# One core, two spectral layers and two feed-forward layers: the input loaded tile by tile, its 16-point matrix on another queue, and a new order table

## The chip, the cores and the metric

The kernel runs on 1 core of one Trainium2 chip. The metric is the device time in microseconds, lower is better. The core has TensorE (PE, and PEld for its weight loads), VectorE (DVE), ScalarE (ACT), GpSimd (POOL) and SyncE (SP). SP's and ACT's instruction streams issue transfers on a queue of their own (SPq, ACTq); GpSimd issues indirect ones.

## The reference

The input x has 2048 rows of 448 bf16 numbers. Two kinds of layer alternate, twice:

```python
def _A_ref(x, w_r, w_i):                       # spectral layer
    X = rfft2(x.astype(float32))               # over 2048 x 448
    return irfft2(X * (w_r + 1j * w_i), s=(2048, 448)).astype(bfloat16)

def _B_ref(x, w1, b1, w2, b2):                 # feed-forward layer, 448 -> 1792 -> 448
    r = relu(x @ w1 + b1)
    return (r * r) @ w2 + b2

x = x + _A_ref(layernorm(x), A_w_r, A_w_i)
x = x + _B_ref(layernorm(x), B_w1, B_b1, B_w2, B_b2)
x = x + _A_ref(layernorm(x), A_w_r, A_w_i)
x = x + _B_ref(layernorm(x), B_w1, B_b1, B_w2, B_b2)
```

## The kernel before, in words

x lies in 16 tiles of 128 partitions x 448; partition p holds rows 16p to 16p+15, and tile t their t-th. The transform over 2048 rows is split into 16 x 128 points. All of it is matrix products with constant matrices.

The first stage ("A1") works tile by tile. VectorE (BN_STATS, then BN_AGGR) or, for tiles 1, 4 and 6, ScalarE (one pass with Copy, one with Square, each with a running sum) takes the mean and variance; ScalarE takes the square root; VectorE its reciprocal (`rstd`). The function `minus` writes -2 times the mean (`m2`). The function `scaled` multiplies the 16-point matrix FA by rstd into a buffer `Fs`. Then come five matmuls: four with x as weights and the scaled matrix as the moving operand, and one with m2 that takes the mean out. These five are called a product here. An evacuation writes the result from PSUM to `XA`. There are four Fs buffers in rotation, so the scaling of tile t waits until the product of tile t-4 has read its buffer.

After that, for eight pairs of frequencies: TD (a transform over the 448 columns, constant TD_sb), B (the 128-point transform, G_sb), W (VectorE's products with the complex weights Wt) and Bi (the transform back, H_sb or HS_sb). TI and AI (TI_sb, FI_sb) finish the way back and add the residual. Then per pair of tiles a layer norm and a transposition into yT (by matmuls with J_sb, or by a transposing transfer), then the first feed-forward matrix (`h`) and the second (`o`). The second half of the kernel repeats all that, with its first stage ("A2") woven into the feed-forward stage.

Every instruction is recorded with what it reads and writes. Instructions that go together form a unit with a tag ("A1.3", "sp.xin"). The table `ORDER` gives each unit of a tag, in the order in which the program recorded them, its rank, and a letter for the engine where there is a choice. Each engine runs its instructions strictly by rank, and so does each queue its transfers. Before the change, `schedule` also keeps a clock of its own with costs and due times, by which it chooses a PSUM bank for each matmul tile and puts dummy matmuls (`warm_mm`, on a block of ones) where it finds TensorE idle while the array would be slow.

Names that the prediction uses: `xin` is the input in SBUF, `x_sb` the running x, whose rows are 512 wide. `x4` is the tile whose landing the constants' transfers wait for. ACT's `warm` instruction is a square root of one number, which makes ScalarE load its table of functions.

Of the kernel before, what the change touches and what calls it, by code (L numbers as in the profile page):

```python
# [10 lines left out]
P = 128  # L11
# [30 lines left out]
def make_constants():  # L42
# [71 lines left out]
    for g, M in enumerate((cl * np.cos(th), cl * np.sin(th))):  # L114
# [1270 lines left out]
```

## Time and profile before

| what | value |
|---|---|
| median of 3 runs | 267.37 us (266.88 to 268.2) |
| span of the profiled execution | 267.8 us |
| instructions | 5840 |
| DMA, whole execution | 17.03 MB, mean 64 GB/s |
| TensorE's granted clock, mean | 1.000 |

The page gives the span of the profiled execution, from its first to its last instruction, and no other time for it. The profile's rows for a stretch of time show the start and length in microseconds, the engine, the line, the operation with what it writes and reads, the count, and in brackets the idle time of the engine just before and what ended it. The rows of busy times by stretch show the length and then, for TensorE, its weight loads, VectorE, ScalarE and GpSimd, the busy time and the number of instructions, then the granted clock, the busy share of the DMA engines and the GB/s they moved. The granted clock stands at 1.00 in all these rows; how fast the array works is read from the distance between the starts of matmuls.

### The profile page before, as it was taken

The numbers are of one execution on the slowest core, as the hardware profiler recorded it, in microseconds if no ns is written. First come the engines' busy times: TensorE is split into PE (matmuls) and PEld (weight loads), VectorE is DVE, ScalarE is ACT, GpSimd is POOL, SyncE is SP. The second block draws the span as 40 slices with busy tenths as digits, with TensorE's granted clock in tenths as the row PEclk, the third lists the DMA queues.
The fourth block names the chain that finished last, engine by engine and source line by source line (L and its number), as shares of the span: only waits on it lengthen the run. The fifth ranks groups of instructions, "written<-read, shape, count | busy, mean of one in ns | idle before, by whom it ended". The sixth has DMA issues, their size and how long they took to land. (4 is left out here: it accounts for less than half of the span.)

```text
span 267.8 us, 5840 instructions
## 1 busy us (share of the span) xinstructions
PE 259.3 (97%) x2194; PEld 158.9 (59%) x2194; DVE 212.7 (79%) x652; ACT 171.3 (64%) x391; POOL 14.4 (5%) x42
## 2 busy tenths in 40 slices
PE   6899999899999999999999999989999999999996
PEld 1477665798544544555559774779654554454554
DVE  5866999899996964999999899899998963463722
ACT  4688994979429755985128896889735753678000
POOL 0577000000000000000000000000000000000000
PEclk9999999999999999999999999999999999999999
DMA  6999370020420222300000000011232026200211
GB/s 222 305 376 354 74 228 17 0 42 10 54 52 2 39 43 44 68 0 0 2 0 4 2 2 0 2 23 22 39 73 42 0 42 111 89 2 0 70 39 47
DMA packets 27312, 17.03 MB, mean 64 GB/s; under 512 B 20210, under 2 KB 25810, under 8 KB 27156
## 3 DMA queue, kind: packets, MB, share of 16 engines
q1 hardware_dynamic: 26692, 14.82, 21.7%
q10 hardware_dynamic: 432, 1.03, 1.1%
q0 software_dynamic: 160, 0.81, 0.8%
q8 instruction: 17, 0.28, 0.5%
q14 instruction: 11, 0.09, 0.1%
HBM read 11.15 MB, written 1.84 MB: 48 GB/s over the span
## 5 line engine op out<-in xcount | busy, mean ns | idle before, releaser
L636 PE MATMUL ps<-yT,W_sb 64*128 64x512 bf16 (+1 forms) x770 | 90.3, 346 | 0.0
L636 PE MATMUL ps<-W_sb,arena 128*128 128x448 bf16 (+2 forms) x490 | 87.5, 336 | 0.0
L636 PEld LDWEIGHTS ps<-yT,W_sb 64*128 64x128 bf16 (+1 forms) x770 | 51.5, 95 | 36.0 <-issue 1.5
L636 PEld LDWEIGHTS ps<-W_sb,arena 128*128 128x128 bf16 x490 | 46.3, 98 | 36.3 <-DVE arena L688 0.8
L655 ACT ACTIVATE arena<-ps,b1col 128x512 bf16<-128x512 f32 x84 | 51.9, 691 | 14.2 <-PE ps L636 14.0
L688 DVE TENSOR_TENSOR arena<-arena 128x512 bf16<-128x512 bf16 (+1 forms) x140 | 45.7, 367 | 18.0 <-ACT arena L655 17.6
L1109 ACT ACTIVATE VT<-x_sb 128x448 bf16<-128x448 bf16 x32 | 18.4, 577 | 13.4 <-DVE x_sb L1085 13.3
L661 ACT ACTIVATE arena<-ps 128x448 bf16<-128x448 f32 (+1 forms) x44 | 25.1, 693 | 2.4 <-PE ps L636 2.2
L1205 DVE SCALAR_TENSOR_TENSOR x_sb<-ps,arena 128x448 bf16<-128x448 f32 (+2 forms) x27 | 15.2, 570 | 14.1 <-PE ps L636 13.7
L655 ACT ACTIVATE mv<-mv,epst 128x1 f32<-128x1 f32 (+1 forms) x46 | 12.6, 294 | 17.2 <-DVE mv L794 12.1
L655 ACT ACTIVATE arena<-ps 128x256 bf16<-128x256 f32 x56 | 17.8, 392 | 4.0 <-PE ps L636 3.7
L661 ACT ACTIVATE XA<-ps 128x512 bf16<-128x512 f32 x29 | 15.6, 592 | 3.2 <-PE ps L636 3.2
L661 ACT ACTIVATE VT<-ps 128x512 bf16<-128x512 f32 (+1 forms) x26 | 13.0, 567 | 7.0 <-PE ps L636 6.9
L636 PE MATMUL ps<-yT,VT 64*128 64x512 bf16 x42 | 15.8, 376 | 0.0
L636 PE MATMUL ps<-HS_sb,arena 128*128 128x512 bf16 x64 | 14.9, 380 | 0.1
L636 PE MATMUL ps<-arena,G_sb 128*128 128x448 bf16 (+1 forms) x76 | 14.4, 333 | 0.5 <-ACT arena L661 0.4
L672 ACT ACTIVATE arena<-x_sb,rstd 128x448 bf16<-128x448 bf16 x11 | 7.2, 666 | 10.5 <-DVE rstd L1124 6.0
L636 PE MATMUL ps<-TD_sb,XA 112*64 112x112 bf16 (+2 forms) x312 | 13.2, 224 | 0.0
L636 PE MATMUL ps<-Fs,xin 128*128 128x256 bf16 x64 | 10.0, 290 | 3.0 <-DVE mv L784 2.9
L636 PEld LDWEIGHTS ps<-TD_sb,XA 112*64 112x64 bf16 (+2 forms) x312 | 12.1, 108 | 1.1 <-issue 0.6
L688 DVE TENSOR_TENSOR tmp<-arena,Wt 128x896 bf16<-128x896 bf16 (+1 forms) x14 | 11.4, 852 | 1.7 <-ACT arena L661 1.5
L1135 DVE SCALAR_TENSOR_TENSOR arena<-x_sb,mv,b2row 128x448 bf16<-128x448 bf16 x16 | 10.7, 679 | 0.1
(76 smaller groups left out, 300.9 us busy)
## 6 DMA issues: line engine op xcount, KB each, us to landing
out_dram<-x_sb SPq DMA_DIRECT2D x15, 112.0 KB, 1.7
W_sb<-in_B_w_dram SPq DMA_DIRECT2D x1, 1568.0 KB, 16.1
W_sb<-in_B_w_dram SPq DMA_DIRECT2D x1, 1344.0 KB, 6.7
HS_sb<-c_HS SPq DMA_DIRECT2D x1, 1024.0 KB, 11.2
G_sb<-c_G SPq DMA_DIRECT2D x1, 960.0 KB
xin<-in_A_x_dram ACTq DMA_DIRECT2D x2, 448.0 KB, 5.4
xin<-in_A_x_dram SPq DMA_DIRECT2D x1, 448.0 KB
Wt<-in_A_w_i_dram SPq DMA_DIRECT2D x1, 392.0 KB, 4.7
```

The costliest lines, as they stand in the source:

```text
L636: return sch.add("pe", lambda e: e.matmul(_res(o), lhsT, rhs, start=start, stop=stop, skip_group_check=skip), [lhsT, rhs], [o], cost=cost, ...
L655: sch.add("act", lambda e: e.activation(o, _res(i), func, **kw), rd, [o], cost=c)
L661: op = sch.add(engs[0], lambda e: e.activation(o, _res(i), ACT.Copy) if h[0].eng == "act" else e.tensor_copy(o, _res(i)), [i], [o], cost=c ...
L672: op = sch.add(engs[0], lambda e: e.activation(o, i, ACT.Copy, scale=s) if h[0].eng == "act" else e.tensor_scalar(o, i, s, 1.0, op0=ALU.mu ...
L688: sch.add(eng, lambda e: e.tensor_tensor(o, _res(a), b, op), [a, b], [o], cost=_free(o) / rate + 69.0)
L1109: sch.add("act", lambda e, i=i, o=o, x=x: e.activation(o, x, ACT.Square, accum_out=mv[:, i, 4:5]), [x], [o, mv[:, i, 4:5]], cost=560.0)
L1135: small(lambda e, o=o, x=x, m=m: e.scalar_tensor_tensor(out=o, in0=x, scalar=m, in1=b2row[:], op0=ALU.add, op1=ALU.add), [x, m, b2row[:]], ...
L1205: small(lambda e: e.scalar_tensor_tensor(out=o, in0=_res(i), scalar=r[0] if r else 1.0, in1=xb[:, t, d0:d1], op0=ALU.mult, op1=ALU.add), [ ...
```

## The change

Four things are changed in the text, and one table.

1. x is loaded in 12 pieces in place of 7: tiles 0 to 7 one by one, the rest in pairs, divided between SP's and ACT's queue. FA goes on ACT's queue.
2. The scaled matrix of tile t is written to `x_sb[:, t, 0:256]`, a place of its own, in place of one of four buffers in rotation.
3. The dummies are listed in a table: 13 of 512 columns and one of 128, ahead of the first product. Before it was nine ahead of the first product and seven between the first and the second.
4. The constants' transfers wait for tile 7, where they waited for tile 4 (which came with 5, 6 and 7).
5. ORDER is new up to the beginning of the first feed-forward stage, and from there on has the old order with all ranks five higher. It now also holds the PSUM bank of each matmul tile (after the colon), so `schedule` only follows the table.

```diff
 ORDER = {
-    "dve.warm": "1", "dve.epst": "4", "sp.xin": "0 12 15 18", "act.xin": "11 14 17", "sp.FA_sb": "13",
+    "dve.warm": "170", "dve.epst": "12", "sp.xin": "17 14 29 10 15 13 11", "act.xin": "7 5 4 0 1", "act.FA_sb": "2",
-    "act.warm": "16", "pool.ones": "8", "pool.back": "10", "dve.x_sb": "3", "dve.W1_sb": "5", "pool.yT": "92 52",
+    "act.warm": "202", "pool.ones": "8", "pool.back": "9", "dve.x_sb": "3", "dve.W1_sb": "6", "pool.yT": "25 24",
...
+WARM = {52: ((7, 512), (7, 512), (7, 512), (7, 512), (7, 512), (7, 512), (7, 512), (7, 512), (7, 512), (7, 512), (7,
+    512), (7, 512), (7, 512), (7, 128))}
...
-        for u in self.ranked():
-            e = u.eng
...
+        for n, u in enumerate(self.ranked()):
+            for b, w in WARM.get(n, ()):
+                d = _Op("pe", self.warm_fn(b, w), False, 0.0, 0.0)
+                take(b, d)
...
-        for n, (a, b, e) in enumerate(((0, 1, "sp"), (1, 2, "act"), (2, 3, "sp"), (4, 8, "act"), (3, 4, "sp"), (8, 12, "act"),
-                                       (12, 16, "sp"))):
+        for n, (a, b, e) in enumerate(((0, 1, "sp"), (1, 2, "act"), (2, 3, "sp"), (3, 4, "sp"), (4, 5, "act"), (5, 6, "sp"),
+                                       (6, 7, "act"), (7, 8, "sp"), (8, 10, "sp"), (10, 12, "act"), (12, 14, "sp"),
+                                       (14, 16, "act"))):
             dma(e, xin[:, a:b, :], x_dram[:, a:b, :])
-            if n == 2:
-                dma("sp", FA_sb[:], dc["FA"])
-            if n == 3:
+            if n == 1:
+                dma("act", FA_sb[:], dc["FA"])
                 sch.add("act", lambda e: e.activation(warm[:, 0:1], warm[:, 0:1], ACT.Sqrt), [warm[:, 0:1]], [warm[:, 0:1]],
                         cost=200.0)
...
-        x4 = [xin[:, 4, :]]
+        x4 = [xin[:, 7, :]]
...
-                x, f = xin[:, t, :], Fs[:, t % NFS, :]
+                x, f = xin[:, t, :], x_sb[:, t, 0:2 * P]
                 scaled(f, FA_sb[:], r, EV["FS"])
```

Three places show what the new table does at the start. The names in brackets are the semaphores that an instruction waits for; `s_sp_dma5` is that of the sixth transfer on SP's queue, counted from 0.

SP's transfers at the start of the program, before:

```order
L628 DMA xin<-in_A_x_dram 128x448 x2
L628 DMA FA_sb<-c_FA 128x256
L628 DMA xin<-in_A_x_dram 128x448
L628 DMA xin<-in_A_x_dram 128x1792
L628 DMA G_sb<-c_G 128x768 [waits s_act_dma1]
L628 DMA Wt<-in_A_w_i_dram 128x2x224
L628 DMA Wt<-in_A_w_i_dram 128x7x224
L628 DMA TD_sb<-c_TD 128x896
```

These are tiles 0 and 2, FA, tile 3, tiles 12 to 15, then the constants. And now, with tile 5, the pairs 12-13 and 8-9, tiles 2, 7 and 0, and behind TD tile 3:

```order
L550 DMA xin<-in_A_x_dram 128x448
L550 DMA xin<-in_A_x_dram 128x896 x2
L550 DMA xin<-in_A_x_dram 128x448 x3
L550 DMA TD_sb<-c_TD 128x896 [waits s_sp_dma4]
L550 DMA xin<-in_A_x_dram 128x448
L550 DMA Wt<-in_A_w_r_dram 128x7x224
L550 DMA G_sb<-c_G 128x3840
```

Tile 0 moved from the first place to the sixth, tile 3 behind a transfer that waits for tile 7.

ScalarE's first instructions, with its queue's transfers (tile 1, tiles 4 to 7, tiles 8 to 11), before:

```order
L628 DMA xin<-in_A_x_dram 128x448
L628 DMA xin<-in_A_x_dram 128x1792
L729 ACT_TABLE_LOAD
L729 ACTIVATE warm<-warm 128x1 [waits s_dve]
L628 DMA xin<-in_A_x_dram 128x1792
L781 ACTIVATE yT,mv<-xin 128x448 [waits s_act_dma0]
L655 ACTIVATE mv<-mv,epst 128x1 [waits s_dve]
```

And now, with the pairs 10-11 and 14-15, FA, then tiles 6, 4 and 1:

```order
L550 DMA xin<-in_A_x_dram 128x896 x2
L550 DMA FA_sb<-c_FA 128x256
L550 DMA xin<-in_A_x_dram 128x448 x3
L701 ACT_TABLE_LOAD
L701 ACTIVATE yT,mv<-xin 128x448 [waits s_act_dma5]
L577 ACT_TABLE_LOAD
L577 ACTIVATE mv<-mv,epst 128x1 [waits s_dve]
```

Tile 1 moved from the first place to the sixth, and a table load now stands between tile 1's first pass and the square root for tile 0 (`mv<-mv,epst`).

VectorE from its first statistics to the first scaled matrix, before:

```order
L793 BN_STATS st<-xin 128x6 [waits s_sp_dma0]
L794 BN_AGGR mv<-st 128x2 [waits s_dve]
L793 BN_STATS st<-xin 128x6 [waits s_sp_dma1]
L794 BN_AGGR mv<-st 128x2 [waits s_dve]
L800 RECIPROCAL rstd<-mv 128x1 [waits s_act]
L805 TENSOR_SCALAR m2<-mv 128x1
L673 TENSOR_SCALAR Fs<-FA_sb,rstd 128x256 [waits s_dve,s_sp_dma2]
```

And now:

```order
L713 BN_STATS st<-xin 128x6 [waits s_sp_dma5]
L714 BN_AGGR mv<-st 128x2 [waits s_dve]
L713 BN_STATS st<-xin 128x6 [waits s_sp_dma3]
L720 RECIPROCAL rstd<-mv 128x1 [waits s_act]
L713 BN_STATS st<-xin 128x6 [waits s_sp_dma7]
L714 BN_AGGR mv<-st 128x2 [waits s_dve]
L713 BN_STATS st<-xin 128x6 [waits s_sp_dma0]
L714 BN_AGGR mv<-st 128x2 [waits s_dve]
L704 SCALAR_TENSOR_TENSOR mv<-mv 128x1 [waits s_act]
L714 BN_AGGR mv<-st 128x2 [waits s_dve]
L720 RECIPROCAL rstd<-mv 128x1 [waits s_act]
L595 TENSOR_SCALAR x_sb<-FA_sb,rstd 128x256 [waits s_act_dma2]
```

The scaled matrix of tile 0 (last row) now stands behind the statistics of tiles 0, 2, 3 (`s_sp_dma7`) and 5 (`s_sp_dma0`), where it stood behind those of tiles 0 and 2.

More of the change, by code (lines that the diff above doesn't have):

```diff
@@ L327 @@
     DMA_RATE = 350.0
-    TURN = (200.0, 100.0)
-    SLACK = 60.0
-    DMA_SLACK = 200.0
-    BEGIN = 800.0
-    WINDOW = 3413.0
     def __init__(self):
@@ L342, in __init__ @@
         self.lead = {}
-        self.warm_from = 0.0
-        self.cold_until = 0.0
-        self.warm_share = 0.7
     def add(self, eng, fn, reads=(), writes=(), is_dma=False, cost=100.0, lat=130.0, unit=None):
@@ L403, in ranked @@
             if u.tag in ORDER:
-                w = ORDER[u.tag].split()[k]
+                w = ORDER[u.tag].split()[k].split(":")
+                for t, b in zip(u.tiles, w[1] if len(w) > 1 else ""):
+                    t.bank = int(b)
+                w = w[0]
                 if w[-1].isalpha():
@@ L415, in schedule, with take @@
     def schedule(self):
-        free = dict.fromkeys(self.ENGINES, self.BEGIN)
-        free["pe"] = self.warm_from
-        bank_free = [0.0] * NB
-        bank_user = [None] * NB
-        dma_free = 0.0
-        rows = 128
-        used = []
-        done = {}
-        def ready(op):
-            r = 0.0
-            for d in op.gdeps:
-                if d.unit is op.unit or (d.eng == "pe" and op.eng == "pe"):
-                    continue
-                if d.is_dma:
-                    r = max(r, done[d] + 130.0 + self.DMA_SLACK)
-                else:
-                    r = max(r, done[d] + d.lat + (80.0 if op.eng == "pe" else 0.0) + (self.SLACK if d.eng != op.eng else 0.0))
-            return r
-        def pick(n, now, taken):
-            best = None
-            for b in range(0, NB, n):
-                if any(i in taken for i in range(b, b + n)):
-                    continue
-                if all(bank_user[i] is None or all(op in done for op in bank_user[i].readers) for i in range(b, b + n)):
-                    f = max(bank_free[b:b + n])
-                    key = (max(f, now), n == 1 and bank_free[b ^ 1] <= now, f)
-                    if best is None or key < best[0]:
-                        best = (key, b)
-            assert best is not None, "no bank is free"
-            return best[1]
-        for u in self.ranked():
-            e = u.eng
-            first = free[e] + (self.TURN[u.rows < 128] if e == "pe" and u.rows != rows else 0.0)
-            taken = []
-            for w in u.tiles:
-                now = max(first, ready(u.ops[0])) + sum(op.cost for op in u.ops[:u.ops.index(w.first)])
-                w.bank = pick(w.n, now, taken)
-                taken += range(w.bank, w.bank + w.n)
+        user = [None] * NB
+        def take(b, op):
+            if user[b] is not None:
+                op.deps.extend(r for r in user[b].readers if r not in op.deps)
+        for n, u in enumerate(self.ranked()):
+            for b, w in WARM.get(n, ()):
+                d = _Op("pe", self.warm_fn(b, w), False, 0.0, 0.0)
+                take(b, d)
+                if not self.ops["pe"]:
+                    d.deps.extend(self.warm_deps)
+                self.ops["pe"].append(d)
             for op in u.ops:
-                t = max(first if op is u.ops[0] else free[e], ready(op))
                 for w in u.tiles:
@@ L461, in schedule @@
                         for i in range(w.bank, w.bank + w.n):
-                            old = bank_user[i]
-                            if old is not None:
-                                t = max(t, bank_free[i] + 80.0 + self.SLACK)
-                                for rd in old.readers:
-                                    if rd not in op.deps:
-                                        op.deps.append(rd)
-                            bank_user[i] = w
-                if e == "pe" and op is u.ops[0]:
-                    while t - free["pe"] >= 120.0:
-                        f = free["pe"]
-                        cold = f < self.cold_until
-                        recent = sum(min(b, t) - max(a, t - self.WINDOW) for a, b in used[-90:] if b > t - self.WINDOW)
-                        if not (cold or recent < self.warm_share * self.WINDOW):
-                            break
-                        n = next((n for n in (512, 256, 128) if (n / 2.4 + 2.5) * (2.0 if cold else 1.0) + 60.0 <= t - f), 0)
-                        if not n:
-                            break
-                        b = min(((bank_free[b], b) for b in range(NB) if b not in taken and (
-                            bank_user[b] is None or all(x in done for x in bank_user[b].readers))), default=None)
-                        if b is None:
-                            break
-                        if b[0] > f:
-                            free["pe"] = b[0]
-                            continue
-                        c = (n / 2.4 + 2.5) * (2.0 if cold else 1.0)
-                        d = _Op("pe", self.warm_fn(b[1], n), False, c, 195.0)
-                        if bank_user[b[1]] is not None:
-                            d.deps.extend(bank_user[b[1]].readers)
-                        if not self.ops["pe"]:
-                            d.deps.extend(self.warm_deps)
-                        self.ops["pe"].append(d)
-                        used.append((f, f + c))
-                        free["pe"] = f + c
-                    t = max(t, free["pe"])
-                    begin = t
@@ L497, in schedule @@
-                t += op.cost
-                free[e] = t
-                done[op] = t
-                self.ops[e].append(op)
-                if op.is_dma:
-                    done[op] = dma_free = max(dma_free, t + 1800.0) + op.lat
-                    if e == "pool":
-                        done[op] = max(dma_free, t + 7000.0)
-                for w in op.takes:
-                    for i in range(w.bank, w.bank + w.n):
-                        bank_free[i] = max(bank_free[i], t + op.lat)
@@ L508, in schedule @@
-            if e == "pe":
-                rows = u.rows
-                used.append((begin, free["pe"]))
-        self.length = max(done.values())
-        self.used = used
-        self.done = done
+                            take(i, op)
+                            user[i] = w
+                self.ops[u.eng].append(op)
         for e in self.ENGINES:
@@ L732, in bass_interleave_layers__spectral_gfnet__dense_activation_squared_relu__prompt_kernel @@
         sch.warm_deps = sch.lead["pool"] = [sch.last_write[k] for k in _pages(ones[:])][:1]
-        sch.warm_from = 1000.0
-        sch.cold_until = 4800.0
         sch.add("pool", lambda e: e.iota(back[:, 0:1], pattern=[[0, 1]], base=(16 * (P - 1) + 9) * 225, channel_multiplier=-16 * 225), [],
```

191 rows, old and new, of the table ORDER are left out of this document.

## Prediction

> **What bounds the kernel now.** I read the busy shares first, then the chain that ended last, then TensorE's busy time by stage, and at last the first 21 us row by row, because that is where the diff works.
>
> ```profile
> PE 259.3 (97%) x2194; PEld 158.9 (59%) x2194; DVE 212.7 (79%) x652; ACT 171.3 (64%) x391; POOL 14.4 (5%) x42
> ...
> 175.25 90.26 PE ps L636 x700
> ```
>
> The last row is a piece of the chain that ended last (start, length, who): its final 90 us are matmuls in a row. A busy TensorE need not be TensorE at its peak, so I ask where it stood still.
>
> ```profile
> 13.00:21.15 8.15, 8.10 (x72) 6.62 (x70) 5.34 (x21) 6.62 (x15) 5.13 (x14) 1.00 1.03 374
> 21.15:46.14 24.99, 24.38 (x179) 15.76 (x177) 22.43 (x37) 19.79 (x39) 4.96 (x13) 1.00 0.58 164
> 46.14:62.00 15.86, 15.08 (x166) 13.35 (x165) 13.92 (x40) 13.65 (x39) 0.00 (x0) 1.00 0.09 18
> 60.00:70.00 10.00, 10.00 (x80) 7.64 (x79) 9.80 (x36) 8.20 (x27) 0.00 (x0) 1.00 0.29 29
> ```
>
> These are stretches from the span's start: length, then busy time of TensorE, weight loads, VectorE, ScalarE, GpSimd. TensorE lacks 0.05 us in the first, 24.99 - 24.38 = 0.61 in the second, 15.86 - 15.08 = 0.78 in the third, and nothing from 60 on. So from 13 us to the feed-forward stage TensorE is the bound, with only 0.61 + 0.78 = 1.39 us to be had from a better order. A start that shifts the first stage shifts everything behind it.
>
> **The start before.** TensorE's rows of the first stage (start, length, engine, line, operation, count, idle before):
>
> ```profile
> 0.98 4.02 PE L1307 MATMUL ps<-ones 128*128 128x512 bf16 x9 [0.98 <-POOL ones L709]
> 7.95 1.01 PE L636 MATMUL ps<-Fs,xin 128*128 128x256 bf16 x4 [2.95 <-DVE mv L784]
> 8.97 3.19 PE L1307 MATMUL ps<-ones 128*128 128x512 bf16 x7
> 11.96 1.06 PE L636 MATMUL ps<-Fs,xin 128*128 128x256 bf16 x4
> 12.81 0.38 PE L636 MATMUL ps<-Fs,m 128*128 128x256 bf16 x1
> 13.02 0.60 PE L636 MATMUL ps<-Fs,xin 128*128 128x256 bf16 x4
> 13.57 0.60 PE L636 MATMUL ps<-Fs,xin 128*128 128x256 bf16 x4
> ...
> 21.15 2.46 PE L636 MATMUL ps<-TD_sb,XA 128*128 128x224 bf16 x24
> ```
>
> The nine dummies follow each other by about 0.43 us. The first product (five matmuls, tile 0) takes 8.97 - 7.95 = 1.02 us; from 13.02 on one takes 13.57 - 13.02 = 0.55. So the array runs at half pace until about 12.8, that is for 12.8 - 7.95 = 4.85 us of unbroken work, and the nine dummies before the 2.95 us pause left no trace of speed at 7.95. The products end, and the next transform starts, at 21.15. The same stage for the other engines and queues:
>
> ```profile
> 0.72 0.87 SPq L628 DMA_DIRECT2D xin<-in_A_x_dram  x2
> 1.64 0.43 SPq L628 DMA_DIRECT2D FA_sb<-c_FA  x1
> 1.65 1.28 ACT L729 ACT_TABLE_LOAD   x1 [1.65 <-PEq L1370]
> 3.31 0.63 DVE L793 BATCH_NORM_STATS2 st<-xin 128x6 f32<-128x448 bf16 x1 [0.28 <-DMA xin<-in_A_x_dram]
> 3.50 0.58 ACT L781 ACTIVATE yT<-xin 128x448 bf16<-128x448 bf16 x1 [0.35 <-DMA xin<-in_A_x_dram]
> 4.19 0.29 ACT L655 ACTIVATE mv<-mv,epst 128x1 f32<-128x1 f32 x1
> 5.84 0.63 DVE L793 BATCH_NORM_STATS2 st<-xin 128x6 f32<-128x448 bf16 x1 [1.69 <-DMA xin<-in_A_x_dram]
> 7.52 0.28 DVE L673 TENSOR_SCALAR Fs<-FA_sb,rstd 128x256 bf16<-128x256 bf16 x1 [0.73 <-DMA FA_sb<-c_FA]
> ...
> 7.74 0.56 SPq L628 DMA_DIRECT2D TD_sb<-c_TD  x1
> 7.92 1.13 DVE L793 BATCH_NORM_STATS2 st<-xin 128x6 f32<-128x448 bf16 x2
> 9.04 0.24 DVE L794 BATCH_NORM_AGGREGATE mv<-st 128x2 f32<-128x6 f32 x2
> ```
>
> Tiles 0 and 1, first on their queues at 0.72, are used at 3.31 and 3.50; tile 2, second on SP's, only at 5.84; the 16-point matrix FA, third, at 7.52, and that wait set the first product. A queue serves its transfers in order, and later places cost about 2 us each. What all of them moved together:
>
> ```profile
> 2.00:3.00 1.00, 1.00 (x4) 0.30 (x2) 0.78 (x1) 0.99 (x2) 0.00 (x0) 1.00 0.86 247
> 3.00:4.00 1.00, 1.00 (x4) 0.36 (x3) 0.68 (x3) 0.65 (x3) 0.00 (x0) 1.00 1.00 316
> 4.00:5.00 1.00, 1.00 (x3) 0.09 (x1) 0.16 (x1) 0.98 (x5) 0.27 (x2) 1.00 1.01 309
> 5.00:6.00 1.00, 0.00 (x1) 0.00 (x0) 0.16 (x1) 0.04 (x1) 0.00 (x0) 1.00 0.88 315
> 6.00:7.00 1.00, 0.00 (x0) 0.00 (x0) 0.75 (x4) 0.28 (x2) 0.19 (x1) 1.00 1.05 411
> 7.00:8.00 1.00, 0.05 (x1) 0.08 (x2) 0.48 (x4) 0.60 (x4) 0.38 (x1) 1.00 0.96 370
> ...
> DMA to landing us min/median/max: 2.6/4.7/6.0
> ```
>
> The last number of a row is GB/s, so 247 + 316 + 309 + 315 + 411 = 1598 KB moved from 2 to 7 us, and 370 in the next. The DMA share is about 1.0 from 3 us on: the engines are full. The last line is for x's loads alone, from issue to landing.
>
> **The change, part by part.** *x tile by tile.* One tile is 2048 x 448 x 2 / 16 = 115 KB. In the new order SP issues tile 5, the pairs 12-13 and 8-9, tiles 2, 7 and 0, then TD, then tile 3; ACT issues 10-11, 14-15, FA, then 6, 4 and 1. The tiles that VectorE and ScalarE ask for first, 0 and 1, are now the sixth on each queue. Up to and with tiles 0 and 1 go 8 tiles on SP (918 KB) and 7 tiles with FA on ACT (868 KB), 1786 KB; by the rows above that is moved at 7 + (1786 - 1598)/370 = 7.5 us. Use comes about 0.4 later: two tiles, 229 KB, are moved at 2 + 229/247 = 2.9 and used at 3.31. So tiles 0 and 1 come at 7.9 instead of 3.3 and 3.5. TD's issue waits for tile 7 (the fifth; 803 + 753 KB moved, 6.9, landed 7.3), and SP stands still until then; tile 3 is queued behind TD, is issued at 7.3 + 0.56 = 7.9 and lands between 2.6 (the least of x's loads) and 4.7 later (their median), 10.5 to 12.6. I take 11.0, near the lower end, since only tiles 0 and 1 and TD's 224 KB are still under way then.
>
> *The statistics.* In VectorE's new order the scaled matrix of tile 0 stands behind the statistics of tiles 3 and 5: BN_STATS of tile 3 (waits for its landing), an aggregate, BN_STATS of tile 5, two more aggregates, a small product and a reciprocal, then the scaling. From the rows: 2 x 0.565 + 3 x 0.12 + about 2 x 0.1 for the small ones (by the aggregates) = 1.7, the scaling 0.28, to the first matmul 0.15 (7.52 + 0.28 to 7.95): 2.1. The first product starts at 11.0 + 2.1 = 13.1, against 7.95.
>
> *The table load.* The Sqrt on a dummy column that loaded ScalarE's table at 1.65, under the first transfers, is moved far behind; a first load still stands there, but a second one now follows tile 1's first statistic and precedes tile 0's Sqrt. Its chain: 7.9 + 0.69 (3.50 to 4.19) + 1.28 + 0.29 = 10.2, just ahead of tile 3's 11.0, so it costs nothing so long as tile 3 is that late; if tile 3 came sooner, 10.2 would be the floor.
> By the Trainium skill, "ScalarE: Activation LUTs", What ACT_TABLE_LOAD costs, a switch of sets also drains the engine, 1.38 us; the load's 1.28 agrees with the row here, no run here shows the drain, and by that page the sum would be about 0.5 us more (7.9 + 0.69 + 2.66 + 0.29 = 11.5 for 11.0).
>
> *Dummies.* 13 of 512 columns and one of 128 now stand ahead of the first product, none between the first and second. Cold, they end at 0.98 + 13 x 0.43 + 0.11 = 6.7. The seven between, 11.96 - 8.97 = 2.99 us, are gone from TensorE's path. But the pause that follows the dummies is now 13.1 - 6.7 = 6.4 us where it was 2.95, and no row shows a warm array that survived a pause. Bounds for the pace: all warm, 16 products x 0.55 + 0.45 of waits between them (the 14 from 13.02 to 21.15 took 8.13, and 14 x 0.55 = 7.7) = 9.3; cold for 4.85 us as at 7.95, which does 4.85/1.05 = 4.6 products, the other 11.4 at 0.55, and the waits: 4.85 + 6.3 + 0.45 = 11.6. I take 11.6, since the row after the shorter pause was cold. The stage ends at 13.1 + 11.6 = 24.7, against 21.15: +3.5.
> The Trainium skill, "TensorE: Matmul & The Clock Gate", Part 1, speaks against the new place of the dummies too: the array falls back to half speed after an idle window of some 3.4 us. The cold row at 7.95 agrees in kind, and by this rule the sum is the 11.6; without it, the 9.3.
>
> *A buffer per scaled matrix* (x_sb's own tile instead of four rotating Fs) takes away VectorE's and GpSimd's waits for matmuls to release a buffer. Between 13.0 and 21.15 TensorE lacked 0.05 us, so its gain is nothing while the array is fed; the 0.45 of waits are its upper bound.
>
> *Constants in a new order.* TD, then w_r, G, the bias (2-byte pieces), w_i, W2, H, and HS behind those. TD and G are due at 24.7 and about 27, and some 2 MB behind x at 300 GB/s are 7 us: hidden. HS comes behind about 8 MB, the gathers among them, at 300 GB/s 27 us and 2 of start, plus about 1.5 in which SP's queue runs dry at tile 7, plus 3.5 for its own 1 MB: 34 us. Its first use was 37.9 and moves to 41. Nothing.
>
> *The order behind the first stage.* Here the waits that a reorder can reach:
>
> ```profile
> 33.26 1.18 PE L636 MATMUL ps<-arena,G_sb 128*128 128x448 bf16 x4 [0.39 <-ACT arena L661]
> 52.09 0.27 PE L636 MATMUL ps<-J_sb,x_sb 128*128 128x128 bf16 x2 [0.64 <-DVE x_sb L688]
> ...
> 25.21 1.61 DVE L688 TENSOR_TENSOR tmp<-arena,Wt 128x896 bf16<-128x896 bf16 x2 [1.55 <-ACT arena L661]
> 44.02 2.48 DVE L662 CAST VT<-ps 128x512 bf16<-128x512 f32 x4
> ```
>
> In the new order H products stand ahead of the 0.39 wait and inverse transforms ahead of the 0.64 one: up to 1.39 us with all small ones. Against it, VectorE's scaling runs without a break from 25.21 to 44.02, and now starts behind one more cast of 0.6. Between 0 and 1.39 I take half, 0.7. From rank 455 on (in the feed-forward stage) the order is the old one; the new PSUM banks there I put at nothing, as TensorE lacks nothing after 60.
>
> *Sum.* +3.5 - 0.7 = +2.8 on the profiled span of 267.8, 270.6. The median of the three runs shown is 267.37, 0.43 below that span: 270.1.
>
> **Rivals.** *Faster.* A queue's transfers might overlap, so that tile 0, issued at 0.72 + 5 x 0.44 = 2.9, lands 2.6 later at 5.5, as a lone one does; tile 7 at 5.1, tile 3 issued at 5.7 and landed at 8.3. Then the first product starts at 10.4; with 3.7 us of pause and a still warm array the stage ends at 10.4 + 9.3 = 19.7, -1.45, with the 0.7: 265.2. The point that decides is tile 3's landing: below about 10 the kernel can win. For it: tiles 0 and 1, on two queues, both came within 2.8 us. Against it: full engines from 3 us and tile 2's 5.84. *No change.* All lands as I say but the array stays warm: 13.1 + 9.3 = 22.4, +1.25 - 0.7, about 267.9. *Later still.* Tile 3 at its 4.7, 12.6, and none of the 1.39: +5.1, 272.4, or the table load sets the start. *The change doesn't do what it says:* FA is third on ACT's queue, not second, and the dummies end 6 us ahead of the product; that is the forecast itself.
>
> **How the numbers follow.** Forecast 0.60, its own range 268.6 to 271.8; later still 0.12; no change 0.17; faster 0.11. The range leaves out a tenth at each end: low 267.2 takes in most of the warm case, high 272.6 the late tile. Half a per cent, 1.3 us, is about what a measurement tells from no change: slower 0.60 x 0.95 + 0.12 = 0.69, same 0.17 + 0.03 = 0.20, faster 0.11.
>
> **What the profile after would show.** First statistic of tile 0 near 8, tile 3's near 11 with idle time put to x's load, a table load near 8.6 to 9.9, first product near 13 at 1.0 us, products of 0.55 only from about 17 to 18, the next transform at 24 to 25, and the 0.39 and 0.64 waits smaller. I am wrong if tile 3's statistic starts before 10, if the first product takes 0.55, or if TensorE's idle time between the stage's end and the feed-forward grows by over 1 us.

## The result, and the profile after

The changed kernel takes 272.08 us (median of 4 runs, 270.93 to 272.67) against 267.77 (median of 4, 266.88 to 268.2): 1.0158 times the time before, 95% interval 1.0127 to 1.019. Its profiled execution has a span of 270.1 us and a time of 271.87.

From the page after, the busy times, the clock granted to TensorE in 40 slices of 6.75 us, and the last long piece of the chain that ended last:

```profile
PE 259.5 (96%) x2192; PEld 163.0 (60%) x2192; DVE 212.6 (79%) x651; ACT 172.3 (64%) x392; POOL 13.4 (5%) x43
...
PEclk9779999999999999999999999999999999999999
...
177.33 90.33 PE ps L558 x700
```

TensorE is busy for as long as before (259.5 against 259.3), and the last 700 matmuls start 2.08 us later than before (177.33 against 175.25). What is lost is lost early, and the second and third slices are the only ones with a clock below 9. TensorE's rows there:

```profile
0.98 5.84 PE L1227 MATMUL ps<-ones 128*128 128x512 bf16 x14 [0.98 <-POOL ones L631]
12.43 1.01 PE L558 MATMUL ps<-x_sb,xin 128*128 128x256 bf16 x4 [5.62 <-DVE rstd L720]
...
13.45 1.06 PE L558 MATMUL ps<-x_sb,xin 128*128 128x256 bf16 x4
...
17.43 0.60 PE L558 MATMUL ps<-x_sb,xin 128*128 128x256 bf16 x4
...
23.44 2.46 PE L558 MATMUL ps<-TD_sb,XA 128*128 128x224 bf16 x24
```

The first product starts at 12.43 after 5.62 us of idle time, each product takes about 13.45 - 12.43 = 1.02 us until the short rows of 0.60 return at 17.43, and the next transform starts at 23.44 (before: 7.95 and 21.15). What the first product waited for, on VectorE, ScalarE and SP's queue:

```profile
7.94 0.63 DVE L713 BATCH_NORM_STATS2 st<-xin 128x6 f32<-128x448 bf16 x1 [4.84 <-DMA xin<-in_A_x_dram]
...
10.43 0.17 DVE L720 RECIPROCAL rstd<-mv 128x1 f32<-128x1 f32 x1 [1.13 <-ACT mv L577]
10.51 0.61 DVE L713 BATCH_NORM_STATS2 st<-xin 128x6 f32<-128x448 bf16 x1
...
12.02 0.46 DVE L595 TENSOR_SCALAR x_sb<-FA_sb,rstd 128x256 bf16<-128x256 bf16 x2
```

```profile
8.12 0.58 ACT L701 ACTIVATE yT<-xin 128x448 bf16<-128x448 bf16 x1 [3.25 <-DMA xin<-in_A_x_dram]
8.60 0.19 ACT L701 ACTIVATION_READ_ACCUMULATOR yT<-xin 128x1 f32 x1
8.80 1.28 ACT L577 ACT_TABLE_LOAD   x1
10.10 0.29 ACT L577 ACTIVATE mv<-mv,epst 128x1 f32<-128x1 f32 x1
```

```profile
7.74 0.43 SPq L550 DMA_DIRECT2D xin<-in_A_x_dram  x1
```

Tiles 0 and 1 arrive for 7.94 and 8.12. The reciprocal of tile 0 then waits 1.13 us for ScalarE, whose table load stands between tile 1's first pass and the square root. Tile 3's statistic (10.51) follows the reciprocal without a wait of its own. Between the stage's end and 62 us:

```profile
23.44:62.00 38.56, 37.82 (x327) 27.57 (x325) 34.55 (x72) 32.69 (x75) 2.20 (x7) 1.00 0.38 115
```

```profile
39.92 6.61 PE L558 MATMUL ps<-HS_sb,arena 128*128 128x512 bf16 x28 [0.27 <-DVE arena L610]
...
54.20 0.22 PE L558 MATMUL ps<-J_sb,x_sb 128*128 128x128 bf16 x1 [0.22 <-DVE x_sb L610]
```

TensorE lacks 38.56 - 37.82 = 0.74 us, where it lacked 1.39.

**The clock, window by window.** From the trace's record of the granted clock I cut the stretches at its changes. In these rows the clock stands behind the busy times; 1.00 in the rows ahead of an execution's first change only means that none had been recorded yet (there, dummies 0.43 apart are at half pace). After:

```profile
6.88:10.29 3.41, 0.00 (x0) 0.00 (x0) 1.32 (x3) 2.14 (x4) 0.93 (x3) 1.00 0.54 143
10.29:17.12 6.83, 4.69 (x23) 3.26 (x24) 6.52 (x29) 5.84 (x21) 5.56 (x15) 0.50 1.06 325
```

Before, cut into the same 3.41 us back from its grant at 13.01:

```profile
2.77:6.19 3.42, 2.23 (x6) 0.50 (x4) 1.42 (x4) 1.89 (x7) 0.27 (x2) 1.00 0.98 314
...
9.60:13.01 3.41, 3.41 (x12) 1.51 (x10) 3.22 (x16) 2.16 (x10) 1.52 (x4) 1.00 1.07 305
```

The clock changes in steps of 3.41 us. After, the dummies earned the full clock at 6.88, 0.06 us after the last of them had ended (0.98 + 5.84 = 6.82); it was held for one window in which TensorE did nothing, and taken back at 10.29, 2.1 us before the first product.

### The profile page after: what moved, and what is told of

It reads as the page before. It is cut to its first block, busy times and chain, and to the rows that moved or that the text cites. A ratio compares the mean times of both kernels' runs of the same rounds, so it can differ in the third digit from the quotient of the medians.

```text
span 270.1 us, 5822 instructions
## 1 busy us (share of the span) xinstructions
PE 259.5 (96%) x2192; PEld 163.0 (60%) x2192; DVE 212.6 (79%) x651; ACT 172.3 (64%) x392; POOL 13.4 (5%) x43
## 5 line engine op out<-in xcount | busy, mean ns | idle before, releaser
L558 PEld LDWEIGHTS ps<-yT,W_sb 64*128 64x128 bf16 (+1 forms) x770 | 54.5, 95 | 33.0 <-issue 1.5
L583 ACT ACTIVATE VT<-ps 128x512 bf16<-128x512 f32 (+1 forms) x27 | 13.8, 584 | 5.0 <-PE ps L558 5.0
L558 PE MATMUL ps<-x_sb,xin 128*128 128x256 bf16 x64 | 11.0, 313 | 5.6 <-DVE rstd L720 5.6
L558 PE MATMUL ps<-TD_sb,XA 112*64 112x112 bf16 (+2 forms) x312 | 13.1, 224 | 0.0
L594 ACT ACTIVATE arena<-x_sb,rstd 128x448 bf16<-128x448 bf16 x10 | 6.5, 664 | 8.6 <-DVE rstd L1044 4.3
L558 PEld LDWEIGHTS ps<-x_sb,xin 128*128 128x128 bf16 x64 | 7.1, 112 | 7.9 <-issue 6.2
L713 DVE BATCH_NORM_STATS2 st<-xin 128x6 f32<-128x448 bf16 x13 | 7.8, 604 | 4.8 <-DMA xin<-in_A_x_dram 4.8
```

The lines of the kernel that those rows point to most:

```text
L558: return sch.add("pe", lambda e: e.matmul(_res(o), lhsT, rhs, start=start, stop=stop, skip_group_check=skip), [lhsT, rhs], [o], cost=cost, ...
L583: op = sch.add(engs[0], lambda e: e.activation(o, _res(i), ACT.Copy) if h[0].eng == "act" else e.tensor_copy(o, _res(i)), [i], [o], cost=c ...
L594: op = sch.add(engs[0], lambda e: e.activation(o, i, ACT.Copy, scale=s) if h[0].eng == "act" else e.tensor_scalar(o, i, s, 1.0, op0=ALU.mu ...
L713: small(lambda e, si=si, xi=xi: e.bn_stats(si, xi), [xi], [si], (c1 - c0) / 0.96 + 69.0)
```

## Experiments

The theory from the result, A: the start alone makes the kernel slower. Tiles 0 and 1 are late because they are sixth on their queues, two chains of nearly equal length (tile 3's transfer, the table load) hold the first product, and the dummies' clock runs out unused. B: one of the other parts does it (the later order, the PSUM banks, the buffers). C, on the size: the free phase of the clock's windows moves either kernel by more than a microsecond from run to run. e1 to e4, e6 and e10 start from the changed kernel, e8 and e9 from e3, e5 and e7 from the kernel before. Ratios are to the kernel before, on the same chip; its medians there were 267.98 (beside e1 to e4), 268.1 (e5 to e8) and 268.02 (e9 and e10), so medians of different experiments can be compared to some 0.3 us.

### e1: the table load early, x's order as changed

```diff
-    "dve.warm": "170", ... "act.warm": "202",
+    "dve.warm": "0", ... "act.warm": "12",
```

> The changed kernel with the dummy square root (and the one-element memset it reads) back ahead of ScalarE's first statistic; nothing else. Theory A (late x sets the start: tile 3 lands at about 10.2 to 10.5 behind TD, the table load is a second chain of the same length): the table load leaves its place at 8.80 to 10.08, tile 3's statistic starts 0 to 0.3 us earlier than 10.51, the time changes by 0 to -0.4 us. Rival (the second table load alone set the first product): tile 3's statistic starts near 9.3 and the time falls by 1.2 us.

Measured: 271.54 us (270.34 to 271.75), ratio 1.0104 [1.0055, 1.0153]: 0.54 below the changed kernel, with spreads of 1.41 and 1.74 that overlap. VectorE's rows:

```profile
9.26 0.15 DVE L720 RECIPROCAL rstd<-mv 128x1 f32<-128x1 f32 x1
10.34 0.63 DVE L713 BATCH_NORM_STATS2 st<-xin 128x6 f32<-128x448 bf16 x1 [0.93 <-DMA xin<-in_A_x_dram]
```

The reciprocal is 1.17 us earlier and the first product only 0.05 (12.38): now tile 3's statistic waits for its transfer, and starts at 10.34 instead of 10.51. The two chains were within 0.2 us of each other, so removing the table load alone gives no more than that: the stage ends at 23.25, 0.19 us earlier.

### e2: x in the order of use, the table load as changed

```diff
-"sp.xin": "17 14 29 10 15 13 11", "act.xin": "7 5 4 0 1",
+"sp.xin": "0 1 2 10 11 12 13", "act.xin": "0 4 5 6 7",
```

> The changed kernel with x's pieces issued in the order in which they are needed (SP: tiles 0, 2, 3, 5, 7, then the pairs 8-9 and 12-13; ACT: tile 1, FA, tiles 4 and 6, then the pairs 10-11 and 14-15); nothing else. Theory A: tile 0's statistic at about 3.4 instead of 7.94, tile 0's square root behind the table load at about 7, first product near 9.3 instead of 12.43; the first stage ends 2.5 us earlier if the array is still cold then, 4.8 earlier if it is not, and the time falls by as much. Rival (full DMA engines: what x gains the rest loses): less than 1 us.

Measured: 268.12 us (268.0 to 269.23), ratio 1.0011 [0.9985, 1.0036], 4.0 below the changed kernel.

```profile
3.28 0.63 DVE L713 BATCH_NORM_STATS2 st<-xin 128x6 f32<-128x448 bf16 x1 [0.18 <-DMA xin<-in_A_x_dram]
...
7.18 0.16 DVE L720 RECIPROCAL rstd<-mv 128x1 f32<-128x1 f32 x1 [2.55 <-ACT mv L577]
```

```profile
9.19 1.01 PE L558 MATMUL ps<-x_sb,xin 128*128 128x256 bf16 x4 [3.62 <-DVE mv L704]
```

With tile 0 first, its statistic starts at 3.28, not 7.94. Now the table load is the longer chain (2.55 us of wait for ScalarE). The order of x's transfers, two entries of the table, is nearly all of the loss. The execution profiled took 268.88 us, and its stage ends at 20.45, 2.99 us earlier than the changed kernel's; the median falls by more, since six of the ten runs took 268.0 to 268.16 and only four, that one among them, 268.88 to 269.23.

### e3: both

> Both edits at once: x in the order of need and the table load ahead of the first statistic. Theory A: tile 0's square root near 6, first product near 8.2, about 1.4 us after the last dummy, so that the clock granted at the end of the dummies may still hold: the first stage ends at about 17.5 (time -5.9 us against the changed kernel, which would beat the kernel before too) or, cold, at 19.8 (-3.6). Rival (the constants then come too late, HS_sb lands at 33.8 and is needed 16.5 us after the stage's end): the gain stops at about 5 us, with a wait ahead of the HS_sb products.

Measured: 266.95 us (266.14 to 267.96), ratio 0.9947 [0.9918, 0.9976].

```profile
8.04 0.60 PE L558 MATMUL ps<-x_sb,xin 128*128 128x256 bf16 x4 [1.31 <-DVE rstd L720]
...
9.74 0.28 PE L558 MATMUL ps<-x_sb,m 128*128 128x256 bf16 x1 [0.56 <-issue]
10.44 1.01 PE L558 MATMUL ps<-x_sb,xin 128*128 128x256 bf16 x4 [0.42 <-POOL x_sb L595]
```

```profile
6.52:9.93 3.41, 1.55 (x12) 0.91 (x10) 3.03 (x15) 3.16 (x12) 2.57 (x5) 1.00 0.96 320
9.93:13.34 3.41, 2.99 (x15) 2.05 (x15) 2.98 (x14) 2.40 (x7) 3.41 (x11) 0.50 1.07 351
```

With both chains cut the kernel is faster than before: the rest of the new table is no loss. The first product is warm, the third cold again: in the window from 6.52 to 9.93 TensorE was busy for 1.55 us only, since it paused for 1.31 us ahead of the first product and for 0.56 ahead of the second one's last matmul.

### e4: dummies up to the first product, all else as changed

```diff
-WARM = {52: ((7, 512), ..., (7, 512), (7, 128))}
+WARM = {52: ((7, 512),) * 40}
```

> The changed kernel with 40 dummies of 512 columns in place of 13 and one of 128, so that TensorE is busy until about 12.4, when the first product can start; nothing else. Theory A (the clock granted at 6.9 was spent in a pause and taken back at 10.3, products were slow until 17.1): all products at 0.55 us, the first stage ends at about 21.5 instead of 23.44, the time falls by 1.5 to 2.2 us. Rival (the products' pace is set by the statistics and scalings that feed them): no gain, waits between the products.

Measured: 270.19 us (270.03 to 270.48), ratio 1.0077 [1.0053, 1.01].

```profile
0.98 10.41 PE L1226 MATMUL ps<-ones 128*128 128x512 bf16 x40 [0.98 <-POOL ones L630]
12.36 0.60 PE L557 MATMUL ps<-x_sb,xin 128*128 128x256 bf16 x4 [0.96 <-DVE mv L713]
```

The dummies end 0.96 us ahead of the first product, which is as late as in the changed kernel, but warm. The stage ends at 21.75 instead of 23.44, and the median falls by 272.08 - 270.19 = 1.9 us. That is what the cold products cost. The 8 runs lie within 0.45 us, where the 4 of the changed kernel span 1.74.

### e5: the kernel before, profiled once more

> The kernel before, unchanged, for a second profile of it. Its runs beside the first experiments had spans of 265.2 to 267.9 us, and the profile shown before had 267.8. Theory C (the clock gate looks at windows of 3.41 us whose phase differs from run to run, and the first profile had a late one): the span is 265.2 to 267.9 by chance, and it goes with the time at which the full clock is granted, 13.0 in the first profile: a span 1.6 shorter has the grant some 3 us earlier. Rival (the spread comes from elsewhere, say from the transfers): the same grant and stage end with another span.

Measured: 268.02 us, span 266.2, against the span of 267.8 that the prediction worked with.

```profile
7.09 0.74 PE L636 MATMUL ps<-Fs,xin 128*128 128x256 bf16 x4 [2.52 <-issue]
...
7.84 3.15 PE L1307 MATMUL ps<-ones 128*128 128x512 bf16 x7
10.83 0.60 PE L636 MATMUL ps<-Fs,xin 128*128 128x256 bf16 x4
```

```profile
6.66 0.29 DVE L673 TENSOR_SCALAR Fs<-FA_sb,rstd 128x256 bf16<-128x256 bf16 x1 [1.04 <-DMA FA_sb<-c_FA]
```

```profile
0.00:3.99 3.99, 3.01 (x8) 1.08 (x9) 2.47 (x6) 1.97 (x4) 0.39 (x5) 1.00 0.50 150
3.99:7.41 3.42, 0.90 (x6) 0.40 (x5) 1.84 (x9) 2.19 (x10) 1.42 (x4) 1.00 0.99 363
7.41:10.82 3.41, 3.41 (x11) 1.36 (x9) 3.13 (x15) 2.52 (x10) 2.46 (x7) 0.50 1.03 302
10.82:19.50 8.68, 8.63 (x76) 7.11 (x75) 6.73 (x28) 7.09 (x17) 5.18 (x14) 1.00 1.04 376
```

The same program ends its first stage at 19.50 instead of 21.15, and its end is earlier by the same 1.6. Two things make up that time, about half each. The first product starts 0.86 us earlier, and that isn't the clock: the 16-point matrix FA was there for 6.66 and not for 7.52, in the same program. The rest is the clock. Here a window that closed at 3.99 with 3.01 us of dummies in it earned the full clock, and the first product fell partly into that (0.74 us in place of 1.01). The window after next, with the second set of dummies, ended at 10.82 and not at 13.01, so the second product is warm (0.60 in place of 1.06). In the execution profiled before, the window that closed at 6.19 held 2.23 us of dummies, and nothing was granted until 13.01. So theory C holds for this kernel only in part: the phase accounts for 0.8 us here, and the landing of a transfer for 0.9.

### e6: the PSUM banks of before, from rank 560 on

The changed kernel with the bank entries of 142 units put back to those that the scheduler of before chose, from about 91 us on.

> The changed kernel with the PSUM banks that the kernel before had, for all units from rank 560 on (142 of them differ), where the order is the old one; nothing else. In the profiles the changed kernel's lag grows by 0.4 us between the feed-forward stage of the first half and the end. Theory D (the new banks there cost that): -0.3 to -0.5 us. Rival (as in the prediction, banks there cost nothing): 0.

Measured: 271.62 us (271.37 to 272.02), ratio 1.0134 [1.0102, 1.0166]. The loss of 0.24 us between 136 and 150 us that the changed kernel has against before is the same with the old banks, and a new wait of 0.34 us opened at 93.8 us, where new and old numbers meet. So the banks are not the cause of those 0.24 us. The median's -0.46 has the size that I had expected of them, but the trace doesn't put it there: in the execution profiled the clock came at 16.25 and the first stage ended at 23.03, 0.41 us earlier than in the changed kernel, and -0.46 is well within that kernel's spread of 1.74.

### e7: own buffers for the scaled matrices, alone

The kernel before, with the one line of the diff that writes the scaled matrix to `x_sb[:, t, 0:2 * P]`.

> The kernel before with one part of the change alone: the scaled matrix of each tile goes into x_sb's own row instead of four rotating buffers. TensorE lacked 0.05 us from 13 us to the stage's end: 0, within 0.3 us. Rival (the releases held up statistics and scalings that matter): -0.3 to -0.5.

Measured: 267.66 us (266.88 to 268.25), ratio 0.999 [0.9964, 1.0016]. Nothing, as forecast.

### e8: e3, fed and kept warm

e3 with 18 dummies of 512, GpSimd's second gather (of w_r) moved later and tile 8's first statistic moved back:

```diff
-"pool.yT": "25 24", ... "A1.8": "45 66 ...
-WARM = {52: ((7, 512), ..., (7, 512), (7, 128))}
+"pool.yT": "64 24", ... "A1.8": "52 66 ...
+WARM = {52: ((7, 512),) * 18}
```

> The changed kernel with x in the order of need and the early table load, and three more edits: 18 dummies of 512 columns so that TensorE is busy until the first product at 8.0, tile 8's statistic on VectorE behind the reciprocals of tiles 5 and 1, and the second gather on GpSimd behind the first three scalings. Theory A: no pause over 0.5 us ahead of or between the products, so the clock stays granted, all products at 0.55: the stage ends at 17.2 to 18, span 263.5 to 264.5, time 265.3 to 266.3, and the spread between runs (1.8 us with the two edits alone) shrinks. Rival (constants become the bound): a wait ahead of the HS_sb products, which land at 33.9 and would be wanted at 34, and a gain of under 0.5 us over the two edits alone (266.95).

Measured: 266.91 us (266.6 to 267.57), ratio 0.9961 [0.9939, 0.9983].

```profile
7.86 0.60 PE L557 MATMUL ps<-x_sb,xin 128*128 128x256 bf16 x4 [0.96 <-DVE rstd L719]
...
11.67 0.28 PE L557 MATMUL ps<-x_sb,m 128*128 128x256 bf16 x1 [0.73 <-POOL m L724]
12.21 0.60 PE L557 MATMUL ps<-x_sb,xin 128*128 128x256 bf16 x4 [0.25 <-POOL x_sb L594]
```

```profile
10.36 1.02 POOL L625 DMA_INDIRECT yT<-in_A_w_r_dram,back  x1 [0.16 <-issue]
```

All products are warm and the runs lie within 1.0 us, but the median is e3's: the time went to 0.73 + 0.25 us of waits for GpSimd, where the gather stood ahead of the means and scalings of tiles 3 and 4. I had expected about 0.6 us less. (e3's profile above, with cold products in it, is of a run of 267.91 us, among its slowest; five of its ten took 266.14 to 266.87. e8's is of one of 266.65.)

### e9: e8 with that gather later still

```diff
-"pool.yT": "64 24"
+"pool.yT": "90 24"
```

> The kernel of e8_fed_and_warm with one number changed: GpSimd's second gather (of w_r into yT), 1.02 us, goes from ahead of the -2-times-mean and the scaling of tiles 3 and 4 to behind the scaling of the pair 8-9. Theory: the waits of 0.73 us for m and 0.25 us for x_sb in the products (11.67 and 12.21 us) come from that gather alone, so they go, the first stage ends at 17.2 to 17.5 in place of 18.21 with the full clock held throughout, and the median falls 0.7 to 1.0 us below 266.91, to 265.9 to 266.3. Rival 1: GpSimd's scaling itself (0.48 us a tile against 0.55 a product) is the limit, the waits come back one or two products later, and the stage ends at 18.0 to 18.3: 266.7 to 267.0. Rival 2: the gathered rows, now asked for some 2 us later, land too late for the complex products, and a wait of 0.5 us or more opens at 20 to 26 us: 266.9 or more.

Measured: 267.17 us (266.92 to 267.47), ratio 0.9957 [0.9938, 0.9976].

```profile
12.64 1.02 POOL L625 DMA_INDIRECT yT<-in_A_w_r_dram,back  x1 [0.16 <-issue]
...
19.08 5.46 POOL L583 COPY Wt<-yT 128x224 bf16<-128x224 bf16 x14 [2.97 <-DMA yT<-in_A_w_r_dram,back]
```

```profile
14.45 0.60 PE L557 MATMUL ps<-x_sb,xin 128*128 128x256 bf16 x4 [0.92 <-issue]
...
31.09 1.05 PE L557 MATMUL ps<-H_sb,arena 128*128 128x256 bf16 x8 [0.68 <-DVE arena L609]
```

My theory here fell. The two waits went, and one of 0.92 us came back behind the gather's new place (14.45), so the stage ends at 18.27, not at 17.3. And GpSimd's copies of w_r, which start at 19.08 (17.58 in e8), come with 0.68 us of wait for VectorE at 31.09 where e8 has 0.18. That the late copies cause it is argued from their time, not shown. In both places tried among the scalings the gather takes 1.02 us of GpSimd's time and brings a wait of 0.7 to 0.9 us for TensorE.

### e10: the changed kernel without dummies

```diff
-WARM = {52: ((7, 512), ..., (7, 512), (7, 128))}
+WARM = {}
```

> The changed kernel with no dummies at all. Theory (dummies that end long before the first product bring nothing, the array starts cold either way): first product at 12.4, at about 1.0 us, full clock after 3.4 us to 6.8 us of work by the free phase of the window, stage end 21.8 to 23.5, median 271.0 to 272.2 against 272.08, the same within 0.5%. Rival: the dummies' first window still counts for something at 12.4, and without them the cold stretch is longer: stage end later than 23.6 and the median above 273.

Measured: 272.13 us (270.81 to 272.39), ratio 1.0131 [1.0097, 1.0165]: the changed kernel's 272.08. The dummies of the change bring nothing.

```profile
12.34 1.01 PE L557 MATMUL ps<-x_sb,xin 128*128 128x256 bf16 x4 [12.34 <-DVE mv L713]
```

```profile
14.63:18.04 3.41, 3.41 (x17) 2.35 (x16) 2.69 (x12) 2.16 (x5) 2.35 (x9) 1.00 1.08 278
```

The clock came at 18.04, 5.7 us after the first product: the rest of the window that was running, and one whole one.

## Why the prediction was right, and where its terms were off

**The direction and the place.** Right: the first stage is where the time goes, and its cause is the order of x's transfers (e2: -4.0 us) with the table load behind it (e3: another -1.2). But the measured 272.08 lies above the band given to this forecast itself (268.6 to 271.8). It is inside the whole range only because that left room for a still later tile 3, and tile 3 came earlier than forecast: the range held it by luck, and the last paragraph here says what the sum lacked.

**Tiles 0 and 1 at 7.9.** Measured 7.94 and 8.12. Adding up the bytes ahead on both queues, at the rates of the profile before, was good to 0.2 us.

**Tile 3 at 11.0 and the first product at 13.1.** Measured: issued at 7.74 (forecast 7.9), landed in time for 10.34 in e1, first product at 12.43. My 11.0 was 0.7 too late, 10.34 being below the range I had given (10.5). And "so it costs nothing" of the table load was wrong by a little: the two chains, forecast to end at 10.2 (the square root) and 11.0 (tile 3), came at 10.10 + 0.29 = 10.39 and 10.34. The reciprocal stands behind the square root, so tile 3's statistic started at 10.51, and it was the load that ended the wait.
The Trainium skill, "ScalarE: Activation LUTs", What ACT_TABLE_LOAD costs, gives 1.38 us of drain beside the load. The rows disagree: the load starts at 8.80, 0.01 us after the last instruction ahead of it ended, and the square root starts at 10.10, 0.02 us behind it.

**Cold products for 4.85 us, stage of 11.6.** Measured: cold from 12.43 to 17.12, 4.69 us; the stage took 23.44 - 12.43 = 11.0. The 0.45 of waits between products that I had added weren't there; cold products are slower than their scaling (0.46 us for two), which would explain it. e4 shows the term by itself: 1.9 us of the median.
The Trainium skill, "TensorE: Matmul & The Clock Gate", Part 1, has the array fall back after an idle window of some 3.4 us; the row from 6.88 to 10.29 is that case. The runs add that the window need not be idle (below).

**Stage +3.5.** Measured +2.3 (23.44 against 21.15): of the 1.2 between, 0.7 is the first product's start and the rest the waits and pace behind it. Against e5, whose time is close to the median of that program, it is +3.9 (23.44 against 19.50).

**Later order -0.7, constants, banks and buffers nothing.** The idle time up to 62 us fell by 1.39 - 0.74 = 0.65. The constants are nothing: the first product with HS_sb, at 39.92, waits for VectorE and not for a transfer. The buffers are nothing (e7). But 0.3 us were given back after 80 us, in the part that I had put at nothing. Most of it is here, on VectorE, before and after:

```profile
143.10 0.18 DVE L794 BATCH_NORM_AGGREGATE mv<-st 128x2 f32<-128x6 f32 x1
143.19 0.23 DVE L673 TENSOR_SCALAR Fs<-FA_sb,rstd 128x128 bf16<-128x128 bf16 x1
```

```profile
144.93 0.18 DVE L714 BATCH_NORM_AGGREGATE mv<-st 128x2 f32<-128x6 f32 x1
145.24 0.25 DVE L595 TENSOR_SCALAR Fs<-FA_sb,rstd 128x128 bf16<-128x128 bf16 x1
```

A scaling starts 0.31 us behind the aggregate instead of 0.09. e6 and e8 show the same gap, e5 and e7 don't, so neither the banks nor the buffers alone make it. Its cause stays open.

**The step that failed: the baseline.** The forecast was +2.8 on the span, and the two profiles show 270.1 - 267.8 = +2.3. The medians show 272.08 - 267.77 = +4.3. The missing 2 us lie in "The median of the three runs shown is 267.37, 0.43 below that span: 270.1". A span isn't a run's time: in every run where both are known the time is 1.75 to 1.87 us longer (271.87 and 270.1 above). So the profile before was of an execution of about 267.8 + 1.8 = 269.6, among the slowest of that program: in 63 runs of it beside the experiments the time goes from 266.62 to 270.04, the span from 264.8 to 268.2, and the median span is 266.3. Time against time, the account closes: +2.3 between the two profiled executions, 269.6 - 267.77 = 1.8 by which the one of before lay above its median, and 272.08 - 271.87 = 0.2 by which the one of after lay below its own, are 4.3. A span that was longer than two of the three times beside it should have told me. What made that execution slow is what e5 shows: FA landed 0.86 us later, and the clock came at 13.01 and not at 10.82.

## What to carry to other kernels

Look up which transfer the first instruction of each engine waits for, and put that one first on its queue: two entries of the order table cost 4 us here, more than everything behind them could win. Where a start is held by two chains of nearly equal length, cut both or expect little (the early table load moved the first product by 0.05 us with the late tiles, and was worth 1.2 us of the median without them). Dummies help only if they end close ahead of the work that they are to warm: 40 that end 0.96 us ahead of it gave 1.9 us, 14 that end 5.6 us ahead of it gave nothing. And before a difference of 1% is forecast from one profile, ask where that execution lies among the runs, time with time and span with span.

## What the runs showed of the hardware

- The clock is decided in windows of 3.41 us with a phase that differs from run to run. From the rows above, a window with 0.90 us of matmuls (e5) or 1.55 us (e3) lost the full clock at its end. In e9 a window with 2.23 us kept it, and its products go on at full pace:

```profile
4.56:7.97 3.41, 2.23 (x11) 0.78 (x8) 1.99 (x11) 3.30 (x13) 1.63 (x4) 1.00 0.98 336
```

  The same 2.23 us, at half clock in the kernel before, earned nothing (2.77 to 6.19). Nor did 2.29 us in e10 (12.34 to 14.63), while 2.75 us earned it in e7, in the window that closed at 3.73. So the least that keeps the clock lies between 1.55 and 2.23 us here, and the least that earns it between 2.29 and 2.75.
- Products that start cold stayed cold for 3.8 us (e6, 12.48 to 16.25), 4.69 (the changed kernel) and 5.70 (e10, 12.34 to 18.04): between one and two windows, by the phase. At half pace half of that time is lost, an estimate of 1.9 to 2.9 us. The starts that stay warm have runs within 0.45 us (e4), 0.55 (e9) and 0.97 (e8); those that start cold have them within 0.65 (e6), 1.41 (e1), 1.58 (e10) and 1.74 (the changed kernel). That the phase makes this spread fits, but wasn't tested by itself.
- A second table load took its own 1.28 us (8.80 to 10.08) and no more: the square root behind it starts at 10.10.
